# A long convolution feeding a soft mixture of experts: the odd step's order of work, and the place of its z and x loads

## The chip, the cores and the metric

The kernel runs on one core of a Trainium2 chip. The time is the device time of one execution in microseconds (us). The engines are TensorE (PE; its weight loads are shown as PEld), VectorE (DVE), ScalarE (ACT), GpSimd (POOL) and SyncE (SP, which here issues nearly all DMAs). One per cent of the time is 8.7 us.

## What is computed

Two stages, float32 throughout. First a causal long convolution per channel, by Fourier transforms:

```python
x: (8, 5696, 128)   h: (5696, 128)
Xf = rfft(x, n=2*S, axis=1); Hf = rfft(h, n=2*S, axis=0)
y = irfft(Xf * Hf, n=2*S, axis=1)[:, :S, :]
```

Then a soft mixture of experts on the 45568 rows of y, with 32 slots (8 experts of 4):

```python
logits = y @ phi
d = softmax over all rows of logits;  slot_input = d.T @ y
slot_out[e] = relu(slot_input[e] @ w1[e]) @ w2[e]
c = softmax over the 32 slots of logits;  out = c @ slot_out
```

## The kernel before

The transform is written as matrix products in two levels (90 x 64 points). Nine sequences pass through it: h as group 0, then the eight batches of x as groups 1 to 8. One loop (line 583) runs over steps t, and a step does a piece of every stage, each stage some steps behind the one before. Even and odd steps have different orders, written out as strings of letters (line 581), one letter for one piece of work (lines 607 to 628). `ORDER_O` is the even step's string, `ORDER_E` the odd step's. All engines take their instructions in this order, and so does SP with the DMAs.

Stage A, for t below 72, eight steps per group. Letter x, `load_x(t + 3)`: two DMAs (320 and 36 KB) bring a piece of the input into one of three x tiles. Letter f, `fold(t + 1, ...)`: POOL makes sum and difference of the tile's two halves (L206) into two of four folded tiles; the folded tiles of step t + 1 are those of step t - 1. Letter X, `first_low(t)`: eight matmul records of PE (L217) for the low rows, two ACT evacuations (L220), two stores to the scratch tensor f of 240 KB each (L226). Letter Y, `first_high(t)`, in odd steps only: sixteen matmul records for the high rows of the steps t - 1 and t, two evacuations, four stores of 120 KB. So the folds of an odd step overwrite what its high rows read.

Stage B, from t = 9 on, one unit in odd steps and two in even steps. Letter P loads gt pieces (512 KB) from f. Letter b: `stage_b1` (products L267, and four DVE operations with the spectrum of h, L285 and L294) of a new unit, then `stage_b2` (products L309, ACT evacuations L315, one store of 512 KB to the scratch tensor z, L318) of the unit before.

Stage C, from t = 27 on, one pair of two steps for each of 32 tiles T, four tiles per batch. Letter z, `load_pair`, in the even step: five DMAs (1024, 128, 128, 128 and 32 KB, L346) from z into the one z tile. Letter 1, in the odd step: `stage_c1(T)`, the inverse transform: a first half (products L365, an ACT copy L374, two DVE operations), then a call of `stage_c4` of an earlier tile (transposes L431, ACT copies and exponentials, a POOL memset L439, a DVE maximum L446, a POOL subtraction L447), then the second half (products L365, an ACT copy L378). Letter w: what `stage_c1` left: two DVE operations and four POOL additions (L384). The remaining letters: 5 (transposes L454), s (softmax), and in the even step 2, 6, d, 3 and m (transposes L393, the exchange with the slots, logits, column maximum).

PSUM banks for X, Y, C1, C4, C5 and b2 come from one ring of four. After step 71 stages B and C run on alone; from step 73 to 80 each step also loads 512 KB of w1 after its letters. From step 80 on a tail with its own order finishes the last tiles, and then the experts and the output follow.

Of the kernel before, what the change touches and what calls it, by code (L numbers as in the profile page):

```python
# [12 lines left out]
AL = mybir.AluOpType  # L13
# [64 lines left out]
def kernel(  # L78
# [24 lines left out]
    nc = tc.nc  # L103
# [3 lines left out]
    E, _, F = moe_w1.shape  # L107
# [12 lines left out]
    NQ = NJ // 2  # L120
# [57 lines left out]
    xs = {}  # L178
# [17 lines left out]
                out=t_[X0 + r.start:X0 + r.stop, :, :, :].rearrange("p s n d -> p s (n d)"), in_=v)  # L196
        xs[c] = t_

    folded = {}

    def fold(c, comp):
        if c not in xs:
            return
        t_ = xs.pop(c) if comp else xs[c]
        y_ = xf[c % 2 * 2 + comp]
        nc.gpsimd.tensor_tensor(out=y_[:, :, :], in0=t_[:, 0, :, :], in1=t_[:, 1, ::-1, :],  # L206
                                op=AL.subtract if comp else AL.add)
        folded[(c, comp)] = y_

    def first_stage(tiles, width):  # L210

        st = apool.tile([P, CH, 2, D], F32, name="fst", tag="fst", bufs=4)
        for G in range(2):
            p = bank()
            for o, (c, comp) in enumerate(tiles):
                k = slice(0, HP) if width == HP else slice(HP, HP + QP)
                nc.tensor.matmul(p[o * width:(o + 1) * width, :], s1[:, comp + G, k],  # L217
                                 folded[(c, comp)][:, :, :].rearrange("p n d -> p (n d)"),
                                 start=True, stop=True)
            nc.scalar.activation(st[:, :, G, :],  # L220
                                 p[:, :].rearrange("p (n d) -> p n d", d=D), AF.Copy)
        for o, (c, comp) in enumerate(tiles):
            g, j = divmod(c, NJ)
            n0 = comp * HALF + CH * j
            k0, n = (0, N1A) if width == HP else (N1A, N1 - N1A)
            nc.sync.dma_start(  # L226
                out=fd[g].rearrange("q a r c d -> (q a) (r c d)")[k0:k0 + n, n0 * 2 * D:(n0 + CH) * 2 * D],
                in_=st[o * width:o * width + n, :, :, :].rearrange("k n c d -> k (n c d)"))
# [2 lines left out]
        first_stage([(c, comp) for comp in range(2)], HP)  # L231

    def first_high(c):

        both = [(c - 1 + i, comp) for i in range(2) for comp in range(2)]
        first_stage(both, QP)
        for b_ in both:
            del folded[b_]

    gs, prods = {}, {}  # L240

# [107 lines left out]
                                    a=2)[r:r + n, j * w_:(j + 1) * w_])  # L349
        zs[T] = t_  # L350

    def stage_c1(T, between):
        t_ = zs.pop(T)
        kr = used if t_ is zn else P
        y_ = ybufs.pop(0)
        ybufs.append(y_)

        def part(v, f):
            k = (2 * v + f) * CH
            return y_[:, k:k + CH, 0:D] if f == 0 else y_[:, k + CH - 1:k - 1:-1, 0:D]  # L360

        def product(o, tab, q):
            p = bank()
            for h_ in range(2):
                nc.tensor.matmul(p[h_ * HP:(h_ + 1) * HP, :], i1[0:kr, tab, :],  # L365
                                 t_[0:kr, h_, o, :, q, :], start=True, stop=True)
            return p[:, :].rearrange("p (n d) -> p n d", d=D)

        def fold_out(even, minus, plus):
            nc.vector.tensor_tensor(out=plus, in0=even, in1=minus, op=AL.add)  # L370
            nc.vector.tensor_tensor(out=minus, in0=even, in1=minus, op=AL.subtract)

        b_, a_ = product(0, 1, 1), product(0, 0, 0)
        nc.scalar.activation(part(0, 0), b_, AF.Copy)  # L374
        fold_out(a_, part(0, 0), part(1, 0))
        between()
        b_, a_ = product(1, 1, 0), product(1, 2, 1)
        nc.scalar.activation(om[:, :, :], b_, AF.Copy)  # L378

        def after():  # L380
            fold_out(a_, om[:, :, :], op[:, :, :])
            for v, o_, eng in ((1, op, nc.gpsimd), (0, om, nc.vector if tail else nc.gpsimd)):
                for part_, sign in ((part(v, 1), AL.subtract), (part(v, 0), AL.add)):
                    eng.tensor_tensor(out=part_, in0=part(v, 0), in1=o_[:, :, :], op=sign)  # L384

        ys[T] = y_
        return after

    def stage_c2(T):
        for k in (3, 1, 0, 2) if tail else (3, 2, 1, 0):  # L390
# [187 lines left out]
    for comp in range(2):  # L578
        fold(0, comp)
    wait_b2 = []  # L580
    ORDER_E, ORDER_O, XAHEAD = "xXYf1wb5s", "zPxXfb26db3m", 3

    for t in range(last_front + 1):
        us = list(units(t))

        def pair(lag):
            T, half = divmod(t - LAG_C - lag, 2)
            return T if half == 0 and 0 <= T < NT else None

        def prefetch(last):  # L590
            nonlocal loaded
            while loaded < len(queue) and queue[loaded][1] <= last:
                load_g(queue[loaded][0])
                loaded += 1

        def slot_b():
            fresh = bool(us)
            if fresh:
                u = us.pop(0)
                stage_b1(u, t < LAG_C or t >= NA)  # L600
                wait_b2.append(u)
            if len(wait_b2) > fresh:
                stage_b2(wait_b2.pop(0))

        T, U = pair(0), pair(2)
        after = []
        work_ = {
            "z": lambda: load_pair(pair(-1)) if pair(-1) is not None else None,
            "x": lambda: load_x(t + XAHEAD) if t < NA else None,
            "p": lambda: prefetch(t + 1) if t % NJ else None,  # L610
            "P": lambda: prefetch(t + 2),
            "q": lambda: prefetch(t + 1),
            "X": lambda: first_low(t) if t < NA else None,
            "Y": lambda: first_high(t) if t < NA and t % 2 else None,
            "f": lambda: [fold(t + 1, comp) for comp in range(2)] if t < NA else None,
            "d": lambda: dispatch(pair(3)) if pair(3) is not None else None,
            "b": lambda: slot_b(),
            "1": lambda: after.append(stage_c1(T, lambda: stage_c4(U) if U is not None else None))
            if T is not None else stage_c4(U) if U is not None else None,
            "w": lambda: [a_() for a_ in after],  # L620
            "2": lambda: stage_c2(pair(1)) if pair(1) is not None else None,
            "6": lambda: stage_c6(pair(5)) if pair(5) is not None else None,
            "5": lambda: stage_c5(U) if U is not None else None,
            "3": lambda: stage_c3(pair(1)) if pair(1) is not None else None,
            "m": lambda: column_max(pair(1)) if pair(1) is not None else None,
            "s": lambda: list(softmax(U)) if U is not None else None,
            "g": lambda: prefetch(t + 1) if t % NJ == 0 else None,
        }
        if t == last_front:
            if pair(-1) is not None:  # L630
                load_pair(pair(-1))
            assert T is None and U is None
            if pair(3) is not None:
                dispatch(pair(3))
            slot_b()
            slot_b()
            slot_b()
            stage_c2(pair(1))
            slot_b()
            assert not us and not wait_b2  # L640
            V = pair(1)
            stage_c6(V - 2)
            stage_c3(V)
            column_max(V)
            break
        for c_ in (ORDER_E if t % 2 else ORDER_O):
            work_[c_]()
        assert not us
        if t == NA:
            lead.close()  # L650
            wts = inner.enter_context(tc.tile_pool(name="wts", bufs=1, side="right"))
            w1s = wts.tile([P, E, F], F32, name="w1s")
        if NA < t <= NA + E:
            nc.sync.dma_start(out=w1s[:, t - NA - 1, :], in_=moe_w1[t - NA - 1])
# [21 lines left out]
    tail["pool"] = cload.enter_context(tc.tile_pool(name="cload", bufs=2))  # L676
    y_ = tail["pool"].tile([P, Q * CH, D + 1], F32, name="y2", tag="y2", bufs=1)

    after = stage_c1(T, lambda: stage_c4(V))
    after()  # L680
    stage_c5(V)
    list(softmax(V))
    nc.gpsimd.memset(y_[:, :, D:D + 1], 1.0)
# [21 lines left out]
    for V in range(T, NT):  # L705
# [10 lines left out]
        N = T + 1 if V == T else V + 2  # L716
        after = None
        if N < NT:
            after = stage_c1(N, lambda: stage_c4(V))
            load_pair(N + 2)  # L720
        else:
            stage_c4(V)
        if after:
            after()
        if V > T:
            placed_c()
        stage_c5(V)
# [8 lines left out]
            list(end)  # L736
        if V == T:
            ybufs.insert(0, y_)
            stage_c1(T + 2, lambda: None)()
            load_pair(T + 4)  # L740
        else:
            for i in range(4 * (V - T - 1), min(4 * (V - T), E), 2):
                nc.sync.dma_start(
                    out=w2s[:, i:i + 2, :, :],
                    in_=moe_w2[i:i + 2].rearrange("e (p c) d -> p e c d", p=P))
    stage_c6(NT - 2)
    assert list(Ls) == [NT - 1] and not (ys or ds or prods or gs or zs or xs or folded or wait_b2
                or kept or landed)


# [129 lines left out]
```

## Time and profile before

| | us |
|---|---|
| median of three runs | 869.77 (869.0 to 874.97) |
| the profiled execution | 869.39 |
| its span, first to last instruction | 867.6 |
| PE busy / DVE / ACT / POOL | 774.3 / 619.5 / 442.6 / 404.3 |
| mean granted TensorE clock | 0.947 |
| DMA, HBM read / written | 142.81 MB / 128.21 MB, mean 314 GB/s |

How to read the lines that follow: the timeline gives the start, the length, the engine, the line, the operation, out<-in, shapes and a count, and in brackets how long the engine was idle before and what ended that. "SPq" is a DMA being issued by SP's sequencer; the transfer itself comes later. The chain of waits is followed back from the last instruction, each piece with its start and length. A wait list names the waiting line, what it waited for, the sum, the number of times and the longest. Busy time of an engine in a stretch is the union of its instructions.

The stages can be told apart by time: steps 0 to 9 run until about 54 us, the first z tile is loaded at 169 us, the last store to f is issued at 634 us, the tail starts about 725 us (the copy of L666 is issued at 725.7 us), and the first output store is issued at 804.8 us.

### The profile page before, as it was taken

The numbers are of one execution on the slowest core, as the hardware profiler recorded it, in microseconds if no ns is written. First come the engines' busy times: TensorE is split into PE (matmuls) and PEld (weight loads), VectorE is DVE, ScalarE is ACT, GpSimd is POOL, SyncE is SP. The second block draws the span as 40 slices with busy tenths as digits, with TensorE's granted clock in tenths as the row PEclk, the third lists the DMA queues.
The fourth block names the chain that finished last, engine by engine and source line by source line (L and its number), as shares of the span: only waits on it lengthen the run. The fifth ranks groups of instructions, "written<-read, shape, count | busy, mean of one in ns | idle before, by whom it ended". The sixth has DMA issues, their size and how long they took to land.

```text
span 867.6 us, 20501 instructions
## 1 busy us (share of the span) xinstructions
PE 774.3 (89%) x7796; PEld 380.7 (44%) x7796; DVE 619.5 (71%) x929; ACT 442.6 (51%) x906; POOL 404.3 (47%) x386
## 2 busy tenths in 40 slices
PE   5889788889999999999999999999998888968993
PEld 1223333234444444444444444444454444444882
DVE  3049867667778778877888788777788895963642
ACT  2433244435555555655565565555544444773541
POOL 4453424245565566656566555555434332671000
PEclk9999999999999999999999999999999898988855
DMA  9899999999999999999999999999997886670898
GB/s 294 258 300 316 299 326 351 324 327 332 341 326 342 334 329 334 337 330 338 339 348 337 335 328 338 337 326 335 316 330 276 286 308 252 245 305 2 338 405 337
DMA packets 156124, 272.46 MB, mean 314 GB/s; under 512 B 12198, under 2 KB 113702, under 8 KB 152885
## 3 DMA queue, kind: packets, MB, share of 16 engines
q1 hardware_dynamic: 155451, 270.85, 90.2%
q8 instruction: 62, 1.02, 0.5%
q10 hardware_dynamic: 576, 0.31, 0.1%
q14 instruction: 35, 0.29, 0.1%
HBM read 142.81 MB, written 128.21 MB: 312 GB/s over the span
## 4 chain that ended last, share of the span: by engine, by line
PE 55%; DMA 20%; DVE 11%; SPq 2%; issue 2%; POOL 1%; ACT 1%; DVEq 0%; ACTq 0%
PE bank L365 13%; PE bank L217 11%; DMA zc<-z 8%; PE bank L309 7%; PE bt L267 7%; PE bank L393 6%; DMA out_dram<-o 4%; DMA xc<-in_x_dram 4%; DMA gt<-f 3%; DVE yf L294 3%; PE bank L480 3%; DVE p L285 2%; DVE bt L285 2%; SPq L346 2%; PE bank L431 2%
## 5 line engine op out<-in xcount | busy, mean ns | idle before, releaser
L206 POOL TENSOR_TENSOR x<-xc 128x512 f32<-128x512 f32 x144 | 180.1, 1275 | 228.5 <-PE bank L217 196.4
L217 PE MATMUL bank<-x,s 128*32 128x512 f32 (+1 forms) x1152 | 227.4, 613 | 16.3 <-POOL x L206 15.4
L315 ACT ACTIVATE zst<-bank 128x512 f32<-128x512 f32 (+1 forms) x184 | 98.7, 586 | 190.5 <-PE bank L309 168.8
L220 ACT ACTIVATE fst<-bank 128x512 f32<-128x512 f32 x216 | 127.5, 598 | 109.5 <-PE bank L217 85.0
L285 DVE TENSOR_TENSOR p<-bt,Hi 128x1024 f32<-128x1024 f32 x96 | 111.3, 1160 | 34.0 <-PE bt L267 33.1
L365 PE MATMUL bank<-zc,i 128*64 128x512 f32 x480 | 117.5, 611 | 10.8 <-DMA f<-fst 6.4
L309 PE MATMUL bank<-yf,vt 64*64 64x256 f32 x1440 | 102.4, 390 | 26.8 <-DVE yf L294 26.8
L217 PEld LDWEIGHTS bank<-x,s 128*32 128x32 f32 (+1 forms) x1152 | 57.0, 124 | 154.3 <-issue 76.1
L294 DVE TENSOR_TENSOR yf<-bt,p 128x512 f32<-128x512 f32 x192 | 119.3, 662 | 3.3
L267 PE MATMUL bt<-gt,wt 64*64 64x256 f32 x1620 | 113.7, 388 | 6.0 <-DMA gt<-f 3.9
L285 DVE TENSOR_TENSOR bt<-bt,Hr 128x1024 f32<-128x1024 f32 x96 | 112.9, 1177 | 0.0
L267 PEld LDWEIGHTS bt<-gt,wt 64*64 64x64 f32 x1620 | 54.0, 132 | 80.9 <-issue 38.0
L384 POOL TENSOR_TENSOR y<-y,op 128x512 f32<-128x512 f32 x64 | 77.5, 1211 | 11.4 <-DVE op L370 8.3
L309 PEld LDWEIGHTS bank<-yf,vt 64*64 64x64 f32 x1440 | 57.0, 135 | 58.0 <-issue 27.8
L370 DVE TENSOR_TENSOR y<-bank,y 128x512 f32<-128x512 f32 x32 | 22.1, 691 | 70.9 <-PE bank L365 70.6
L393 PE MATMUL bank<-ident,y 109*128 109x109 f32 x512 | 66.1, 283 | 0.7 <-DVE y L384 0.7
L384 POOL TENSOR_TENSOR y<-y,om 128x512 f32<-128x512 f32 x54 | 64.1, 1186 | 2.1
L365 PEld LDWEIGHTS bank<-zc,i 128*64 128x64 f32 x480 | 31.2, 137 | 74.6 <-issue 45.9
L393 PEld LDWEIGHTS bank<-ident,y 109*128 109x128 f32 x512 | 55.9, 154 | 16.5 <-issue 11.1
L395 ACT ACTIVATE yt<-bank 128x360 f32<-128x360 f32 x128 | 51.7, 489 | 4.2 <-PE bank L393 4.2
L833 PE MATMUL op<-so,cT 32*128 32x128 f32 x704 | 45.8, 378 | 3.6 <-ACT o L842 2.9
L285 DVE TENSOR_TENSOR p<-bt,turn 128x1024 f32<-128x1024 f32 (+1 forms) x12 | 14.2, 1179 | 46.6 <-PE bt L267 45.7
(97 smaller groups left out, 817.3 us busy)
## 6 DMA issues: line engine op xcount, KB each, us to landing
gt<-f SPq DMA_DIRECT2D x99, 512.0 KB
z<-zst SPq DMA_DIRECT2D x88, 512.0 KB
f<-fst SPq DMA_DIRECT2D x144, 240.0 KB
zc<-z SPq DMA_DIRECT2D x30, 1024.0 KB
xc<-in_x_dram SPq DMA_DIRECT2D x64, 320.0 KB
f<-fst SPq DMA_DIRECT2D x144, 120.0 KB
out_dram<-o SPq DMA_DIRECT2D x16, 1024.0 KB
zc<-z SPq DMA_DIRECT2D x90, 128.0 KB
```

Of the source, the lines that this page charges most:

```text
L206: nc.gpsimd.tensor_tensor(out=y_[:, :, :], in0=t_[:, 0, :, :], in1=t_[:, 1, ::-1, :], op=AL.subtract if comp else AL.add)
L217: nc.tensor.matmul(p[o * width:(o + 1) * width, :], s1[:, comp + G, k], folded[(c, comp)][:, :, :].rearrange("p n d -> p (n d)"), start=Tr ...
L220: nc.scalar.activation(st[:, :, G, :], p[:, :].rearrange("p (n d) -> p n d", d=D), AF.Copy)
L267: nc.tensor.matmul(bt[q * HP:(q + 1) * HP, a, o, :], wt[r, 2 * i + q, :], t_[r, 2 * o + q, :, :].rearrange("p c d -> p (c d)"), start=True ...
L285: nc.vector.tensor_tensor(out=p_, in0=pv, in1=h_, op=AL.mult)
L294: eng.tensor_tensor(out=y_[r, 0:k, c, :], in0=pv[:, :, c, :], in1=pi[r, 0:k, 1 - c, :], op=op_)
L309: nc.tensor.matmul(bz[q][a * HP:(a + 1) * HP, o * 2 * D:(o + 1) * 2 * D], vt[r, i, a, :], y_[r, a * m + o, :, :].rearrange("p c d -> p (c ...
L315: nc.scalar.activation(st[:, 0:m, q, :], bz[q][:, 0:m * 2 * D].rearrange("p (o x) -> p o x", o=m), AF.Copy)
L365: nc.tensor.matmul(p[h_ * HP:(h_ + 1) * HP, :], i1[0:kr, tab, :], t_[0:kr, h_, o, :, q, :], start=True, stop=True)
L384: eng.tensor_tensor(out=part_, in0=part(v, 0), in1=o_[:, :, :], op=sign)
L393: nc.tensor.transpose(p[:, i * TR:(i + 1) * TR], ys[T][0:TR, k * CH + i, 0:D], ident[0:TR, 0:TR])
L395: nc.scalar.activation(yt[:, k * CH:(k + 1) * CH, :, :], of_tokens(p), AF.Copy)
```

## The change

The odd step's order becomes "Yf14jXwb5sZx" instead of "xXYf1wb5s". That is: high rows, folds, the first half of C1, C4, the second half of C1, low rows, the remainder of C1, b, 5, s; and at the end the z load for the next odd step and the odd step's x load. The z load moves from the head of the even step to the end of the odd step before it (letter Z), except for the first tile of each batch (T a multiple of 4), which stays with the even step's z and then stands behind the odd step's x load. `stage_c1` becomes a generator that is advanced three times (letters 1, j and w) instead of taking a function to call between its halves. The table `folded` is replaced by a function that names the tile. The even step's order stays as it is. In the tail the generator is advanced so that the work comes in the same sequence as before.

```diff
-        folded[(c, comp)] = y_
+    def folded(c, comp):
+        return xf[c % 2 * 2 + comp]
...
-    def stage_c1(T, between):
+    def stage_c1(T):
...
         fold_out(a_, part(0, 0), part(1, 0))
-        between()
+        yield
         b_, a_ = product(1, 1, 0), product(1, 2, 1)
         nc.scalar.activation(om[:, :, :], b_, AF.Copy)
...
         ys[T] = y_
-        return after
+        yield
+        after()
+        yield
...
-    ORDER_E, ORDER_O, XAHEAD = "xXYf1wb5s", "zPxXfb26db3m", 3
+    ORDER_E, ORDER_O, XAHEAD = "Yf14jXwb5sZx", "zPxXfb26db3m", 3
...
+        def early(V_):
+            if V_ is not None and V_ % NQ:
+                load_pair(V_)
+
+        c1 = stage_c1(T) if T is not None else iter(())
         work_ = {
-            "z": lambda: load_pair(pair(-1)) if pair(-1) is not None else None,
+            "z": lambda: load_pair(pair(-1)) if pair(-1) is not None and pair(-1) not in zs else None,
+            "Z": lambda: early(pair(-2)),
...
-            "1": lambda: after.append(stage_c1(T, lambda: stage_c4(U) if U is not None else None))
-            if T is not None else stage_c4(U) if U is not None else None,
-            "w": lambda: [a_() for a_ in after],
+            "1": lambda: next(c1, None),
+            "4": lambda: stage_c4(U) if U is not None else None,
+            "j": lambda: next(c1, None),
+            "w": lambda: next(c1, None),
...
-    after = stage_c1(T, lambda: stage_c4(V))
-    after()
+    after = stage_c1(T)
+    next(after)
+    stage_c4(V)
+    next(after)
+    next(after)
```

## The prediction

> **What bounds the kernel now.** I read the page first (engine shares, forty slices, DMA queues), then busy time by stage, then the timeline of one turn in the opening stage and of one pair in the middle, then the waits of SP's queue and the chain of waits. The page:
>
> ```profile
> PE 774.3 (89%) x7796; PEld 380.7 (44%) x7796; DVE 619.5 (71%) x929; ACT 442.6 (51%) x906; POOL 404.3 (47%) x386
> ...
> PE   5889788889999999999999999999998888968993
> ...
> DMA  9899999999999999999999999999997886670898
> ...
> q1 hardware_dynamic: 155451, 270.85, 90.2%
> ```
>
> The reader is to see two full resources at once: from slice 10 to 30 both PE and the DMA engines stand at 9, and one queue (SP's) carries nearly all bytes. Shares by stage (length, then busy time of PE, PEld, DVE, ACT, POOL, then PE clock, DMA share, GB/s):
>
> ```profile
> 27.51:36.40 8.89, 7.16 (x33) 1.75 (x33) 0.00 (x0) 3.58 (x6) 4.93 (x5) 1.00 0.83 253
> 108.00:169.00 61.00, 51.49 (x496) 20.30 (x499) 42.52 (x49) 26.50 (x47) 20.02 (x16) 0.94 1.00 335
> 320.02:402.11 82.09, 80.34 (x828) 37.35 (x825) 64.92 (x100) 47.89 (x99) 47.53 (x44) 1.00 0.97 334
> ```
>
> (1) Opening stage (steps 0 to 9, forward transform only): neither PE (7.16 of 8.89) nor DMA (0.83, 253 GB/s) is full. (2) Steps 17 to 26: the DMA engines are full (1.00, 335 GB/s) and PE idles 9.5 us of 61. (3) Steady pairs: DMA 0.97 at the same 334 GB/s, while PE idles only 1.75 us in four pairs. The opening turn, in the timeline:
>
> ```profile
> 26.20 4.93 POOL L206 TENSOR_TENSOR x<-xc 128x512 f32<-128x512 f32 x4 [3.96 <-PE bank L217]
> ...
> 31.18 3.79 PE L217 MATMUL bank<-x,s 128*64 128x512 f32 x22 [0.15 <-POOL x L206]
> ...
> 35.08 4.94 POOL L206 TENSOR_TENSOR x<-xc 128x512 f32<-128x512 f32 x4 [3.96 <-PE bank L217]
> ```
>
> This is a closed loop: four folds (4.93), then the odd step's low rows and high rows back to back (3.79), and only then may the next folds overwrite the tiles that the high rows read: 4.93 + 3.79 and some 0.17 of hand-over make the 8.89 turn. A steady pair:
>
> ```profile
> 428.68 1.08 ACT L315 ACTIVATE zst<-bank 128x512 f32<-128x512 f32 x2 [2.08 <-PE bank L309]
> ...
> 433.37 3.38 SPq L346 DMA_DIRECT2D zc<-z  x5
> ...
> 438.90 3.79 PE L217 MATMUL bank<-x,s 128*64 128x512 f32 x24
> ```
>
> SP issues the z load 3.6 us after the last store before it had its data (429.76). It waits for older transfers, as SP's own waits between 225 and 600 us say (total, times, longest):
>
> ```profile
> SPq L195 <- DMA zc<-z: 23.2, 20, 2.7
> SPq L318 <- DMA gt<-f: 22.7, 17, 2.2
> ...
> SPq L226 <- ACT zst L315: 4.0, 10, 0.6
> ```
>
> So transfers pass in SP's order, always behind a backlog. How tight that is for the z tile, the chain of waits shows where it leaves PE:
>
> ```profile
> 455.99 6.44 DMA zc<-z
> 462.43 0.02 issue
> 462.44 0.51 DMA f<-fst
> 462.95 1.94 PE bank L365 x8
> ```
>
> The last z piece lands and the C1 product starts 0.5 us later.
>
> **The change part by part.** No instruction is added or removed; the `folded` table and the generator form of C1 cost no instruction: 0. In the tail the generator is stepped in the old sequence: 0. I add to the profiled execution's 869.39 us (span 867.6 and 1.8 around it), 0.4 below the median 869.77.
>
> *High rows first, folds after them.* In the opening stage the low rows (half of 3.79, so 1.9 us) leave the loop: they run while POOL folds. The turn becomes 4.93 + 1.9 + 0.17 = 7.0, if the x tiles are there. But the odd step's x load now stands behind its six f stores. Counted from the start of the high rows: 1.9 + 1.9 (both products) + 0.6 (L220 evacuation) + 0.8 (two issues, 0.4 each) = 5.2 until it is issued. Its fold belongs to the next turn, and that turn's high rows wait for the four folds (5.0). With L from issue to landing, two turns take 10.2 + L. L, from below: 3.7, where the turn stays 7.0. From above: 8.3, the longest x load in the chain of waits (160.50 us, in the full stage), giving a turn of 9.2, so no gain. I take the nearest row: the kernel's first x loads are issued at 1.97 and the first fold starts at 7.06, so 5.1, and the turn is 7.65. Four turns follow from 17.30 on (26.20 and 35.08 above, 43.97 next), so 4 x 1.24 = 5.0, and half of one product (0.9) on the very first odd step: 5.9. The DMA engines cap that: from 18.6 to 45.3 us they moved 315, 253 and 256 GB/s in three turns, 7.33 MB; at the full stage's 335 GB/s that is 21.9 us instead of 26.7. Taken: -4.8, the cap, since a full DMA stage follows. Ends: 0, and -7.1 if the rate may be the 374 GB/s of the 9 to 18 us stretch.
>
> The Trainium skill (DMA: Bandwidth & Descriptors, Anatomy of one DMA — SWDGE (gpsimd) path) fits a transfer as about 2.0 us plus bytes over 436 GB/s, which for the 320 KB piece is an estimated 2.75 us; no run here shows an x load that short. By it the turn would be 7.0 and the gain before the cap 8.4, after the cap the same 4.8. The same page (section Rules for kernel authors) says to issue a load early and wait for it late, and this speaks against the change, which issues an x load later by most of a step; by that rule taken alone the opening gain would be 0.
>
> *x load behind the z load, in the full stage.* The same bytes in the same queue at 335 GB/s: 0. Cover: an x tile is folded half a pair and the high rows after its issue (some 8 + 1.9 us there) against 8.3, and the rows made of it are stored some 5 us after that; beyond the cover each late us would first eat PE's idle 9.5 us. Bounds: joining loads to loads may change the rate, by at most the whole transfer of the moved x load, 356 KB at 334 GB/s = 1.1 us per pair, either way. Five pairs: -5 to +5.
>
> *C1 earlier, z load earlier.* C1 stands 1.9 us earlier in PE's order, since only the high rows are ahead of it; its z tile comes 1.1 us earlier, since the x load leaves the front of it (every fourth pair, the first of a batch, keeps the old place: 0). So z is 0.8 to 1.9 us later against its use, and the 0.5 us seen above does not cover that: PE waits at C1. But the queue is full either way (0.97), so PE's wait shifts PE against the queue once and is not paid again in each pair. The low rows, b1, b2 and C5 queue behind the waiting C1; their stores are next due behind three gt loads, two x loads and nine stores (4.4 MB, some 13 us at 334 GB/s), against 9 us of PE and ACT work from C1's start to the last z store's data, so the queue does not run dry. Taken: 0 over the 20-odd steady pairs. Ends: -6.6 (all of PE's idle time between 214 and 624: 410 less 403.36) and +0.8 per pair, the second rival.
>
> *Moves with one answer.* The DVE half of C1 ("w") now stands behind the low rows: DVE has nothing of those, 0. X's first PSUM bank must be emptied by DVE (2 x 0.69) under C4 and C1's second half (0.6 + 1.9): covered. POOL's odd fold starts 1.9 us earlier or waits for the x load behind z; queued behind it are the mask memset, the row subtraction (C5 and the softmax need them) and four y additions (C2 needs them). POOL idles 6.1 us before that fold now; without that cover each late us would be paid in C2. ACT does C1's copies before X's: 0. After step 72 the z load goes ahead of a 512 KB weight load; PE's waits for z in 624 to 724 are 0.9 us: -0.4 taken.
>
> Sum: 869.4 - 4.8 - 0.4 = 864.2.
>
> **The rivals.** *No gain comes through.* The later x load makes POOL wait in place of the PE product. For it: x loads carry 28.9% of the chain between 120 and 175 us. Against it: that is the full stage; in the opening one POOL waits only for PE. Time: 869, within 866 to 872.
>
> *The pairs gain too.* Loads next to loads let the queue run faster until PE alone is the bound: 6.6 us of idle time less 1.75 for the waits on DVE (0.35 per four pairs, five times) is -4.8, giving 859, and with -5 in the full stage 854. For it: gains of that kind need only 1% of rate. Against it: nothing in the profile separates a load's time behind a store from one behind a load.
>
> *Slower: the wait at C1 recurs in every pair.* Place: L365's first product, for its z tile. Price 0.8 us x 28 pairs = 22, with the opening gain 869.4 - 4.8 + 22 = 887; half of the pairs would give 876. It decides when the z load's issue follows its own step's PE work and no longer older transfers: when the 3.6 us between the last z store's data and the z issue fall to zero. Against it: SP's longest wait for an ACT store there is 0.6 us.
>
> **How the numbers follow.** Forecast (opening gain, pairs unchanged) 0.50, about 860 to 867.5; no gain 0.16; pairs too 0.18; slower 0.16. One per cent (8.7 us: what a measurement here tells from no change) puts the borders at 861.1 and 878.5. Faster by over 1%: 0.16 of the pairs' case and 0.06 of the forecast's lower end, 0.22. Slower: 0.12 of the last rival. The rest, 0.66, lies within. The range 857 to 877 leaves out the far ends of both outer rivals, about 0.1 each.
>
> **What would show it.** In the opening stage POOL's folds of four should start every 7.0 to 7.7 us instead of 8.89, with more than 0.95 DMA share, and the step in which x of batch 0 is loaded should be some 5 us earlier. In the pairs PE should show its idle time before L365 and nowhere else, of the old size in sum; 20.3 us from pair to pair, 82 per four. Wrong would be: folds that wait for x loads by several us, a DMA share under 0.95 between 108 and 620, or idle time before L365 near 0.8 us in every pair.

## The result, and the profile after

The changed kernel takes 899.52 us (median of 4 runs, 896.20 to 902.63), the kernel before 869.78 (4 runs, 869.00 to 874.97): ratio 1.0328, 95% interval 1.0273 to 1.0383. It is 3.3% slower, where 864.2 us was forecast. The profiled execution took 902.63 us (span 900.8), 33.2 more than the one of before; it is the slowest of the four. Line numbers after L206 are one to five lower than before: L206 is still the fold, L216 the first stage's products, L225 its stores, L248 the gt load, L341 the z load, L360 the C1 products.

The page (engine shares, DMA slices, queue):

```profile
PE 772.4 (86%) x7796; PEld 383.2 (43%) x7796; DVE 632.2 (70%) x929; ACT 442.5 (49%) x906; POOL 403.8 (45%) x386
...
DMA  9899999999999999999999999999999877771798
...
q1 hardware_dynamic: 155451, 270.85, 90.8%
```

PE has the same busy time (772.4 for 774.3), the queue the same 155451 packets and 270.85 MB. The row of nines in the DMA slices is no shorter, and a slice is longer. So the time is neither in more work nor in an idle queue. The page's mean rate says where it is: 302 GB/s, before 314.

The time goes between the first C1 product and the last ones. From the starts of C1's groups in the trace: the first one starts at 180.0 us (before 177.0), from there to that of the 30th tile it takes 593.8 us (before 563.9), and the rest takes 127.0 (before 126.7). That is +3.0, +29.9, +0.3. The stage view of twenty steady pairs, from the third pair's C1 to the 23rd's, first before, then after (columns as in the prediction: length, busy PE, PEld, DVE, ACT, POOL, PE clock, DMA share, GB/s):

```profile
218.42:627.33 408.91, 401.91 (x4121) 186.93 (x4121) 324.59 (x500) 239.90 (x496) 237.67 (x220) 1.00 0.97 334
```

```profile
223.93:658.82 434.89, 405.76 (x4121) 194.06 (x4121) 335.98 (x497) 239.75 (x495) 237.28 (x220) 0.97 0.98 314
```

A pair grows from 20.45 to 21.74 us. The bytes of a pair are the same (408.91 x 334 / 20 and 434.89 x 314 / 20 are both 6.83 MB), and so is the share of time in which the DMA engines hold a packet. Only the rate fell, by 6%, and the length of a pair grew by 6%. (PE's granted clock is 0.97 in these pairs, before 1.00; e2 below has 0.99 and pairs just as long, so the clock is not what makes them longer.) PE shows it as idle time before C1; of the groups of the page (busy, mean ns, idle time before and what ended it), first before, then after:

```profile
L206 POOL TENSOR_TENSOR x<-xc 128x512 f32<-128x512 f32 x144 | 180.1, 1275 | 228.5 <-PE bank L217 196.4
...
L365 PE MATMUL bank<-zc,i 128*64 128x512 f32 x480 | 117.5, 611 | 10.8 <-DMA f<-fst 6.4
```

```profile
L206 POOL TENSOR_TENSOR x<-xc 128x512 f32<-128x512 f32 x144 | 180.1, 1273 | 235.3 <-DMA xc<-in_x_dram 153.9
...
L360 PE MATMUL bank<-zc,i 128*64 128x512 f32 x480 | 127.2, 655 | 41.4 <-DMA zc<-z 39.6
```

C1's idle time grows from 10.8 to 41.4 us, and POOL's folds, which PE released before, now wait for x loads too. SP's own waits between 225 and 600 us (total, times, longest):

```profile
SPq L248 <- DMA zc<-z: 28.8, 23, 2.9
SPq L313 <- DMA gt<-f: 24.5, 18, 2.4
...
SPq L225 <- ACT fst L219: 6.9, 13, 1.2
```

SP waits above all for older transfers, as before, and seldom for data (a first-stage store 13 times in some 17 pairs, 0.5 us each). And one z load in the chain of waits (start, length, what); it is a batch's first, issued directly behind the odd step's x load:

```profile
434.06 0.60 SPq L341
434.66 0.04 issue
434.70 6.81 DMA zc<-z
441.51 0.14 issue
441.64 2.64 PE bank L360 x8
```

The last z piece lands 6.8 us after its issue, and the chain then goes on through C1.

### The profile page after: what moved, and what is told of

It reads as the page before. It is cut to its first block, busy times and chain, and to the rows that moved or that the text cites. A ratio compares the mean times of both kernels' runs of the same rounds, so it can differ in the third digit from the quotient of the medians.

```text
span 900.8 us, 20428 instructions
## 1 busy us (share of the span) xinstructions
PE 772.4 (86%) x7796; PEld 383.2 (43%) x7796; DVE 632.2 (70%) x929; ACT 442.5 (49%) x906; POOL 403.8 (45%) x386
## 3 DMA queue, kind: packets, MB, share of 16 engines
q1 hardware_dynamic: 155451, 270.85, 90.8%
q8 instruction: 62, 1.02, 0.5%
## 4 chain that ended last, share of the span: by engine, by line
PE 50%; DMA 31%; DVE 8%; SPq 5%; issue 2%; ACT 1%; POOL 1%; DVEq 0%; POOLq 0%; ACTq 0%
DMA zc<-z 13%; PE bank L360 13%; PE bank L216 12%; PE bt L262 7%; PE bank L304 5%; DMA z<-zst 5%; DMA out_dram<-o 4%; DMA gt<-f 4%; SPq L341 4%; PE bank L390 4%; DMA xc<-in_h_dram 2%; PE bank L428 2%; DVE p L280 2%; PE bank L477 2%; DVE bt L280 2%
## 5 line engine op out<-in xcount | busy, mean ns | idle before, releaser
L206 POOL TENSOR_TENSOR x<-xc 128x512 f32<-128x512 f32 x144 | 180.1, 1273 | 235.3 <-DMA xc<-in_x_dram 153.9
L216 PE MATMUL bank<-x,s 128*32 128x512 f32 (+1 forms) x1152 | 221.9, 604 | 13.6 <-POOL x L206 13.2
L360 PE MATMUL bank<-zc,i 128*64 128x512 f32 x480 | 127.2, 655 | 41.4 <-DMA zc<-z 39.6
L216 PEld LDWEIGHTS bank<-x,s 128*32 128x32 f32 (+1 forms) x1152 | 58.1, 124 | 139.2 <-issue 81.1
L360 PEld LDWEIGHTS bank<-zc,i 128*64 128x64 f32 x480 | 33.1, 145 | 108.9 <-issue 86.9
L465 POOL TENSOR_TENSOR L<-L,rs 128x512 f32<-128x512 f32 x32 | 33.6, 1049 | 53.1 <-DVE rs L464 37.7
L844 PE MATMUL op<-so,cT 32*128 32x128 f32 x704 | 43.5, 361 | 5.9 <-ACT o L853 5.4
```

Source lines behind the costliest of these rows:

```text
L206: nc.gpsimd.tensor_tensor(out=folded(c, comp)[:, :, :], in0=t_[:, 0, :, :], in1=t_[:, 1, ::-1, :], op=AL.subtract if comp else AL.add)
```

## The experiments

All kernels are the changed kernel with the edit shown; `E` is the odd step's order, `O` the even step's. For comparison, before is E "xXYf14jwb5s" in these letters with O "zPxXfb26db3m", and the change is E "Yf14jXwb5sZx" with the same O. The ratio of each is against the kernel before, with its 95% interval. "Pair" is the length of one pair in the profiled execution, over the same twenty pairs as above; "C1 wait" is PE's idle time before C1 products per pair, there too.

**One part at a time.** Three theories stood at the start. M: loads that stand next to loads slow the full queue. E: C1 stands earlier, so PE waits for z in each pair. W: between z and gt the x load takes two of the places among the transfers that SP keeps outstanding (each of the 64 DMA issues of SP that the trace of before ties to a landing between 240 and 560 us followed the landing of the eighth DMA before it), so gt comes late.

```diff
 e1  E "xYf14jXwb5s"    new engine order, loads as before
 e2  E "XYf14jwb5sZx"   old engine order, loads as in the change
 e3  E "Yf14jXwb5sxZ"   the change, but x ahead of z
 e4  E "Yf14jxXwb5sZ"   the change, but x between the stores of Y and X
```

> The new engine order alone: the x load is back at the head of the odd step, and the z load stands in SP's order where it stood before. Theory M (joining the x load to the z and gt loads slows the queue, 334 to 312 GB/s in the pairs): 860 to 870 us, the pairs at 82 us per four and 332 to 337 GB/s again. Rival E (C1 comes earlier than its z tile, and PE's wait there recurs in every pair): 890 us or more, PE idle before the C1 product about as large as after the change (27 us between 240 and 640). In the opening stage the x load is early again, so both let the folds of four start every 7.0 to 7.7 us and the first gt load come some 5 us before 46.9.

Measured: 884.35 us, 1.0165 (1.0107 to 1.0223); pair 21.01, 325 GB/s, C1 wait 1.02.

> The old engine order (low rows, high rows, folds, C1) with the z load and then the x load at the end of the odd step. Theory M, and rival W (the x pair between z and gt takes two of eight places for transfers under way, so that gt loads are issued late): 890 to 900 us, 309 to 322 GB/s in the pairs. Rival E: 866 to 872 us, 332 GB/s or more.

Measured: 899.87 us, 1.0352 (1.0315 to 1.0389); pair 21.75, 314 GB/s at share 0.97, C1 wait 1.37.

> The changed kernel with the x load just ahead of the z load at the end of the odd step instead of just behind it. All loads are still next to each other, but gt follows z at once. Theory M: still 890 to 900 us. Rival W: 865 to 875 us. Rival E: 895 to 905 us, since z lands 1 us later still.

Measured: 892.37 us, 1.0283 (1.0229 to 1.0337); pair 21.35, 320 GB/s, C1 wait 1.35.

> The changed engine order with the odd step's x load between the stores of the high rows and those of the low rows, and z at the end of the step. Theory M and rival W: 860 to 870 us, 332 GB/s or more in the pairs. Rival E: 890 us or more.

Measured: 888.94 us, 1.0205 (1.0159 to 1.0251); pair 21.16, 321 GB/s, C1 wait 1.12.

The stage line of e2, to be held against the two above:

```profile
223.24:658.29 435.05, 405.68 (x4121) 188.42 (x4121) 324.87 (x500) 238.94 (x494) 237.75 (x220) 0.99 0.97 314
```

What follows: moving the loads costs the change's whole loss, with C1 at its old place (e2), so E is not needed for it. The engine order alone costs half of it (e1), and the two do not add. W explains a part at most: with x taken out of the gap between z and gt (e3) 22 of 30 us remain. M in its first form did not foresee e1, nor e4, for which M and W both said 860 to 870 us.

**Where e1's time comes from.** e5 keeps only the rows' order, e9 and e16 give the stores their old order in SP's queue by keeping the high rows' four stores back until the low rows' two are issued.

```diff
 e5   E "xYfX14jwb5s"   C1 behind both parts of the first stage again
 e9   E "xYf14jXwb5s"   as e1
 e16  E "xYfX14jwb5s"   as e5
+    def first_stage(tiles, width, hold=False):      # e9 and e16 alone
...
+        if hold:
+            held.append(store)
+            return
+        store()
+        while held:
+            held.pop()()
```

> The old place of the C1 product (behind both first-stage parts), the x load at the head of the odd step and the z load where it was; of the change only the order high rows, low rows is left, so that the queue of SP has the same order as in e1 (884 us). If e1's loss comes from C1 standing earlier on TensorE, this is 868 to 873 us, as before. If it comes from the order of the stores in the queue, it is 880 to 888 us.

Measured: 883.03 us, 1.0120 (1.0050 to 1.0191); pair 21.19, 322 GB/s, C1 wait 0.98.

> The engine order of e1 (high rows, folds, C1, low rows), x load at the head of the odd step, z load where it was; the high rows' four stores are kept back and issued behind the low rows' two, so that the queue of SP has the order of the kernel before. Theory store order (e1's 14 us come from which stores stand last before z): 866 to 873 us, 4096-byte packets near 175 ns as in before. Theory compute order (the later low rows on TensorE and ScalarE hold SP up): 880 to 888 us again.

Measured: 878.09 us, 1.0079 (1.0039 to 1.0119); pair 20.70, 330 GB/s, C1 wait 0.94.

> e9 with the C1 product behind both parts of the first stage, as before: what is left of the change is that TensorE and ScalarE take the high rows first, while the queue of SP has the order of before. If e9's 8 us come from C1's place: 868 to 873 us. If from the rows' order on the engines: 876 to 882 us.

Measured: 870.10 us, 0.9979 (0.9953 to 1.0005); pair 20.39, 335 GB/s, C1 wait 0.34.

The twenty pairs of e5 and of e16, which differ in the order of six stores alone:

```profile
224.99:648.84 423.85, 403.18 (x4120) 190.85 (x4121) 349.12 (x500) 239.55 (x495) 235.31 (x218) 0.99 0.97 322
```

```profile
215.38:623.21 407.83, 398.53 (x4120) 189.73 (x4121) 349.64 (x502) 239.87 (x496) 235.81 (x219) 1.00 0.98 335
```

The same bytes, nearly the same share, 322 against 335 GB/s: which stores stand last before z is worth 1.4% of the whole (1.0120 against 0.9979). The two profiles put 16 us of it into these 408, but e5's profiled execution, 890.96 us, is the slowest of its four, and the medians differ by 13. That the high rows go first on the engines costs nothing (e16). With the stores kept back, C1's earlier place costs 1.0% (e9 against e16), and e9's 0.94 us against 0.34 of C1 wait in each pair is where it shows. All six stores then wait for the low rows behind C1: between 240 and 560 us SP waits 8.7 us for the data of first-stage stores in e9 and 1.9 in e16. With the stores in their new order the same move of C1 costs nothing that can be seen: e5 and e1 take 883.03 and 884.35 us, with pairs of 21.19 and 21.01, and e2 and the change, which differ in the whole engine order, 899.87 and 899.52. Neither of the two expected values of e9 was met; it lies between them.

**Where the x load stands.** With the old engine order, the odd step's x load moves nearer to z.

```diff
 e6   E "XxYf14jwb5s"                        between low and high rows' stores
 e7   E "XYf14jxwb5s"                        behind both, ahead of one store
 e10  E "XYf14jwb5sZx"  O "zPXxfb26db3m"     e2, even step's x behind the stores
 e11  E "XYf14jwb5s"    O "zPuxXfb26db3m"    odd x behind gt in the even step
+            "u": lambda: load_x(t + XAHEAD - 1) if 0 < t <= NA else None,
 e18  E "XYf14jwb5sZx", O from the first C1 on "zXPxfb26db3m"
```

> Order of the kernel before, but the odd step's x load stands between the low rows' and the high rows' stores. Theory mix (loads cost more when they stand next to other loads in the full queue, less between stores): 866 to 873 us, 2048-byte packets near 99 ns. Theory nearness (the closer the odd x load comes to the z load, the dearer): a part of e2's 30 us by its place, 875 to 882 us.

Measured: 872.73 us, 1.0005 (0.9971 to 1.0038); pair 20.70, 331 GB/s.

> Order of the kernel before, but the odd step's x load stands behind the high rows' stores and before the zst store. Theory mix: 866 to 875 us, since a store still lies between it and z. Theory nearness: 882 to 895 us, nearly e2's 900.

Measured: 882.85 us, 1.0135 (1.0096 to 1.0174); pair 20.99, 325 GB/s.

> e2 (old engine order, odd step's x load behind z; 900 us) with the even step's x load taken out of the row of loads and put behind the low rows' stores. The row of loads is then ten long again (z 5, x 2, gt 3), as in before, and only its order is other. Theory row length (many loads in a row lower the rate): 868 to 876 us. Theory nearness to z (x's packets beside z's are what costs): 890 to 900 us.

Measured: 888.55 us, 1.0223 (1.0154 to 1.0292); pair 21.09, 324 GB/s.

> Order of before, but the odd step's x load stands behind the gt loads of the next even step, directly ahead of that step's own x load: the row of loads is as long as in e2 (twelve), but no x load is a neighbour of z. Theory row length: 893 to 903 us as e2. Theory nearness to z: 868 to 876 us.

Measured: 900.85 us, 1.0349 (1.0281 to 1.0418); pair 21.61, 316 GB/s at share 0.96.

> e2 (old engine order, odd step's x load behind z; 900 us) with the low rows' two stores between z, x and gt, x from the first C1 on: rows of seven and five loads in place of one of twelve. Theory row length: 868 to 878 us. Theory nearness (x's packets beside z's are what costs): 885 to 900 us, at least e10's 888.

Measured: 892.24 us, 1.0254 (1.0203 to 1.0305); pair 21.54, 317 GB/s at share 0.96.

With seven, five and one transfers between the odd x load and the z load (before, e6, e7), and with x directly behind z (e2), a pair takes 20.45, 20.70, 20.99 and 21.75 us: the nearer, the dearer, though the first of these steps is not clear of noise in the times (e6: 1.0005). The new order of the stores gives a second row: with seven, three and no transfers between x and z (e1, e4, e3), and with x behind z (the change), a pair takes 21.01, 21.16, 21.35 and 21.74 us. A row of loads broken by stores helps little while x stays beside z (e18 takes back some 8 of e2's 30 us, against the 868 to 878 us of row length); a row of the old length takes back 11 (e10, which falls between both theories). e11 looked like the proof of row length, but its waits (240 to 560 us) show another cause:

```profile
POOL x L206 <- DMA xc<-in_x_dram: 76.8, 8, 11.2
...
PEld bank L451 <- POOL dt L436: 16.9, 8, 3.5
```

Its x load is issued a step later than before, the folds wait for it, POOL's memset dt queues behind the fold, and PE waits for POOL (0.94 us a pair before L451) and not for z. So e11's time does not separate the two theories. The lengths of its packets say that nearness to z is not all: although no x load stands near z, the rate for the time in which the DMA engines hold packets is 316/0.965 = 328 GB/s (before 334/0.973 = 343), and x's packets (2048 bytes) take 123.7 ns on average over the twenty pairs, as in e2 (123.6). With one of the two x loads between stores and one behind gt they take 99.4 (before), with both between stores 89.3 (e8, below). So x's packets are slower the more of the x loads stand beside other loads, whether z or not.

**Loads spread, and a load left out.**

```diff
 e8   E "xXYf14jwb5s"   O "zPXxfb26db3m"
 e13  E "xXYf14jwb5s"   O "zXPxfb26db3m"
 e14  E "xXYf14jwb5s"   O "zXPfbx26db3m"
 e15  E "nXYf14jwb5s"   O "zPxXfb26db3m"
+            "n": lambda: xs.setdefault(t + XAHEAD, xcs[(t + XAHEAD) % len(xcs)]) if t < NA - XAHEAD else None,
```

> Order of the kernel before, but in the even step the x load stands behind the low rows' stores instead of behind the gt loads. Theory mix: the x load leaves a row of seven or eight loads, so its packets get shorter: 855 to 866 us. Theory that only the window of eight in front of z counts: same, 867 to 873 us. If later x loads are late for POOL's folds, slower: 875 to 885 us, with POOL waiting for xc.

Measured: 867.68 us, 0.9968 (0.9937 to 0.9999); pair 20.38, 336 GB/s, first C1 at 180.7.

> Order of before, but in the even step the low rows' two stores stand between the z loads and the gt loads. Theory row of loads (more than five loads in a row lower the rate, shorter rows are better): 855 to 866 us. Theory row of stores: 867 to 874 us. If gt now comes late for the B products: 875 to 890 us with TensorE waiting for gt.

Measured: 885.94 us, 1.0169 (1.0150 to 1.0188); pair 20.67, 330 GB/s, first C1 at 187.2.

> Order of before, but the even step's loads are spread: z, low rows' stores, gt, one zst store, x. Theory row of loads: 853 to 866 us. Theory row of stores: 866 to 874 us. If gt comes late: 875 to 890 us.

Measured: 874.71 us, 1.0053 (1.0021 to 1.0086); pair 20.36, 333 GB/s, first C1 at 186.2.

> Order of before with the odd step's x loads left out (33 of 72 chunks; the folds read old data, so part of the input is not read). The row of loads stays ten long; the row of stores between gt and the next z is twelve long, as in e2. Theory row of loads: the rate stays at 332 to 341 GB/s and the bytes left out save about 1.0 us a pair of steps, 832 to 845 us. Theory row of stores: the rate falls to about 312 GB/s as in e2 and eats the saving, 862 to 875 us.

Measured: 852.33 us, 0.9773 (0.9750 to 0.9795); pair 20.15. Its twenty pairs:

```profile
209.17:612.13 402.96, 401.19 (x4124) 185.84 (x4120) 324.72 (x500) 239.48 (x495) 237.94 (x220) 1.00 0.94 322
```

PE is busy for 401.19 of 402.96 us and never waits for z: 20.15 us is PE's floor for a pair, and the queue, at share 0.94, has room. Before stands 0.3 us above that floor; from the first C1 to the 30th tile's it takes 563.9 us and e15 555.9, so with this engine order the most that another order of the loads could have gained in the pairs is 8 us. The rate for the time the DMA engines hold packets stays that of before (322/0.945 = 341, before 334/0.973 = 343, after 314/0.978 = 321 GB/s), although the stores here stand twelve in a row. So a long row of stores is not what lowers it, at least where the queue has room. e13 and e14 lose 9 to 10 us before the first C1, where PE now waits 9.6 and 7.4 us for gt (between 60 and 177 us; before 3.9), and in the pairs spread loads bring next to nothing (20.67 and 20.36, for 20.45; per busy share 339 and 343 GB/s). That speaks against row length. e8 comes out between 867 and 873 us, as the theory of the window in front of z said.

**Parts put together.** e12 is e9 with e8's O; e17 is e16 with e8's O from the first C1 on and the old O ahead of it.

```diff
 e12  E "xYf14jXwb5s"   O "zPXxfb26db3m", stores kept back
 e17  E "xYfX14jwb5s"   O "zPxXfb26db3m", stores kept back
+    ORDER_P = "zPXxfb26db3m"
+        for c_ in (ORDER_E if t % 2 else ORDER_O if t < LAG_C else ORDER_P):
```

> e9 with the even step's x load behind the low rows' stores (e8's edit). If store order is what cost e1 its time and e8's gain of 0.3% adds, 862 to 868 us; if compute order costs, 878 to 888 us.

Measured: 879.16 us, 1.0104 (1.0060 to 1.0147); C1 wait 0.79 a pair, near e9's. The time is that of the second expectation.

> e16 (high rows first on the engines, stores in the old order; 870 us, its first C1 at 174.8 us where before has 177.0) with e8's edit (even step's x load behind the low rows' stores) only from the first C1 product on; in e8 the stretch from the first C1 to that of the 29th pair took 560.8 us, in before 563.9. If both hold and add: 174.8 + 560.8 where before has 740.9, 863 to 867 us. If the two don't add: 868 to 873 us.

Measured: 865.76 us (12 runs) against 871.95 (17 runs), 0.9936 (0.9903 to 0.9968). It beats both kernels, the one of before by 0.6%. Its profiled execution does not show where: pairs of 20.44 us and the first C1 at 176.1, for 20.45 and 177.0.

## Why the prediction was wrong

*"x load behind the z load, in the full stage. The same bytes in the same queue at 335 GB/s: 0."* This is the step that failed, together with the like words of "C1 earlier, z load earlier", "Taken: 0 over the 20-odd steady pairs". Its own bound of 1.1 us per pair was near the mark: measured +1.3 (e2: 21.75 against 20.45), 26 us over the twenty pairs, and e2's first C1 starts 3.8 us later besides. As a limit the bound was wrong in kind: it counted the moved load's own transfer alone, and more than half of the growth is in other transfers' packets (below). And the bound was put only on five pairs of the full stage, and in the steady pairs the sum stood at 0 up to a rival at 0.8 us. The text even said that nothing in the profile separates a load's time behind a store from one behind a load. An unknown that the profile can't separate applies in every pair in which the queue is full: x is still loaded in some 22 of the pairs (t from 27 to 71), and 22 x 1.1 = 24 us either way would have made the range 840 to 888, which still leaves out 899.5. By parts, the sum had -4.8, 0 and -0.4 us up to the first C1, in the pairs and behind them; the profile has +3.0, +29.9 and +0.3.

*"But the queue is full either way (0.97), so PE's wait shifts PE against the queue once and is not paid again in each pair."* In the change itself nothing speaks against it: e2, with C1 at its old place, takes as long as the change, in the pairs too (21.75 and 21.74 us). But as a rule it does not hold: with the stores kept back, C1's earlier place costs 0.31 us a pair (e9 20.70, e16 20.39), 6 us over the twenty pairs, in a queue nearly as full; the medians differ by 8.0. The third rival (0.8 us in every pair, 887 us) named the symptom, idle time before L360 in every pair. Its condition, that the z load's issue no longer follows older transfers, did not arise: SP waits for transfers as before, and e2, with C1 at its old place, already has 1.37 of the change's 1.46 us of C1 wait a pair: it comes with the lower rate.

*High rows first, folds after them: -4.8.* The loop was read rightly, but two terms were off, and the change got nothing of the gain. The odd x load is issued 6.7 us after the high rows begin and not 5.2 (their first weights load at 29.89, the issue is at 36.61), since SP issues the low rows' stores first and waits for their data; it lands 5.2 to 5.7 us later (taken: 5.1; the estimate of 2.75 us by the skill's fit is half of that). Two turns take 17.2 us for the 15.3 worked out, so 8.6 each, near the 8.89 of before:

```profile
25.50 4.93 POOL L206 TENSOR_TENSOR x<-xc 128x512 f32<-128x512 f32 x4 [4.24 <-DMA xc<-in_h_dram]
32.65 4.94 POOL L206 TENSOR_TENSOR x<-xc 128x512 f32<-128x512 f32 x4 [2.22 <-DMA xc<-in_h_dram]
42.70 4.93 POOL L206 TENSOR_TENSOR x<-xc 128x512 f32<-128x512 f32 x4 [5.11 <-DMA xc<-in_x_dram]
```

With the x load at its old place (e1) the loop does close faster, with turns of 6.9 to 7.7 us, and the folds get seven us ahead. Then the gain is not handed on:

```profile
45.42 2.50 POOL L206 TENSOR_TENSOR x<-xc 128x512 f32<-128x512 f32 x2 [1.28 <-PE bank L216]
56.78 2.50 POOL L206 TENSOR_TENSOR x<-xc 128x512 f32<-128x512 f32 x2 [8.86 <-DMA xc<-in_x_dram]
```

The first gt load waits until the stores of step 7 have landed, of which the low rows' are now last. It is issued at 47.17 us (before 46.87), and the next x load stands behind it. With the old order of stores (e16) gt is issued at 45.13 and the first C1 starts at 174.8 for 177.0: 1.7 to 2.2 us of the 4.8 show there. The change itself starts its first C1 3.0 us later than before. The rule that the prediction weighed against this step, to issue the DMA early (the Trainium skill, DMA: Bandwidth & Descriptors, Rules for kernel authors), gave 0 for the opening stage. The trace agrees with it so far: turns of 8.6 us with the x load issued late (the change), 6.9 to 7.7 with it issued early (e1). That e1's early load did not bring its first C1 forward (181.7 us) is the stores' doing: with them in their old order and all else the same (e9) it starts at 176.7.

*The moves with one answer* held as far as e16 tests them: where the high rows go first on every engine, DVE, ACT and POOL cost nothing. POOL's fold does wait for the x load in the change (88.0 us between 225 and 600), and that is not paid on PE, whose idle time in the pairs stands before C1 alone; in e11 it is paid. The -0.4 us after step 72 did not come: from the 23rd tile's C1 to the 29th's it takes 110.1 us, before 108.7.

*The rivals.* "The pairs gain too" had the right stake (the rate of the queue) and the wrong sign. "No gain comes through" was true of the opening stage and said nothing of the pairs.

*What stays open* is why the same packets take longer. The trace's packet records between 240 and 560 us give the means: packets of 2048 bytes (x) 98.7 ns before, 120.5 after, of 4096 (f stores) 173.8 and 185.5, of 16384 (z) 706 and 738; in e5 100.9, 189.8 and 736. The quickest tenth is the same everywhere (84, 159 and 611 ns); the slow ones became more, with the slowest tenth of the f stores' packets from 201 ns before, 275 after and 304 in e5. Added up by size over the twenty pairs, and divided by the 16 engines, packet time per pair grew from before to e2 by 0.51 us in packets of 1024 bytes (gt loads and z stores, 9.10 to 9.61), 0.46 in x's (1.88 to 2.34), 0.17 in the f stores' and 0.12 in z's: 1.3 in all, the whole growth of a pair. In e5 it grew in the f stores' (4.17 to 4.57) and z's (4.07 to 4.21) alone. So which packets take longer depends on which transfers stand side by side; the trace doesn't say at what point of the path they meet. The Trainium skill (DMA: Bandwidth & Descriptors, Why a DMA increments its semaphore by 16 and not by 1) says that a transfer uses as many engines as the largest number up to 16 that divides the slowest dimension of both its sides, for DMAs of SP's kind (HWDGE) the lowest-numbered ones. By that rule, as an estimate, a z piece of eight rows would use eight engines and an f store of 30 or 60 rows fifteen. No run here shows it, since the records don't name the engine of a packet. Other cuts of the z load were not tried.

## What to carry to other kernels

In a queue that is full all the time, the order of transfers is a cost of its own: measure the rate per busy share of the stage (here 343, 333 and 321 GB/s in before, e5 and the change, for the same bytes), and treat the rate as unknown as soon as a transfer gets other neighbours, in every turn of the loop. A busy share that stays at 0.97 says nothing about that. When a change joins several moves, undo the moves one by one: here taking the high rows first was harmless with the stores left as they were (e16), and the moved x load alone made a loss as large as the whole change's (e2). And look for the loss in the packets of the other transfers too, not only of the one that was moved.

## What the runs showed of the hardware

The rate of the full queue changed by 7% (336 GB/s in e8, 314 in e2) with the order of the same transfers, at a busy share of 0.97 in both. The position of two x pieces, 356 KB of 6.83 MB in a pair, is worth 1.3 us in 20.4, more than their whole transfer at 334 GB/s (1.1 us). The order of six small stores ahead of the z load is worth 4% of that rate (335 to 322 GB/s). Packets of 2048 bytes in the x loads took 89.3 ns on average with both loads between stores (e8), 99.4 with one of them behind other loads (before) and 121 to 124 with both beside other loads (the change, e2, e11).
